# Where the weight pieces of a fused mLSTM and SwiGLU kernel land: other homes for pieces 2 to 6, and one half moved from ACT's queue to SP's

## The chip, the cores and the metric

The kernel runs on one core of a Trainium2 chip. Its engines are TensorE (PE in the profile; PEld is its weight load), VectorE (DVE), ScalarE (ACT), GpSimd (POOL) and SyncE (SP). Sixteen DMA engines move data; in this kernel the transfers are issued by SP (queue q1 of the profile) and by ACT (queue q10). The metric is the device time in microseconds (us), the median over runs.

## The reference

Two blocks follow each other. The first is an mLSTM cell over 4 batches, 8 heads, 768 positions and a head size of 40. The second is a SwiGLU block on 3072 tokens of 320 features, with 1536 hidden features.

```python
for t in range(S):
    m_new = np.maximum(f_gate[:, :, t] + m, i_gate[:, :, t])
    f_stab = np.exp(f_gate[:, :, t] + m - m_new)
    i_stab = np.exp(i_gate[:, :, t] - m_new)
    C = f_stab[..., None, None] * C + i_stab[..., None, None] * np.einsum('bhd,bhe->bhde', vt, kt)
    n = f_stab[..., None] * n + i_stab[..., None] * kt
    h_tilde = np.einsum('bhde,bhe->bhd', C, qt)
    denom = np.maximum(np.abs(np.einsum('bhd,bhd->bh', n, qt)[:, :, None]), 1.0)
    y[:, :, t] = h_tilde / denom / (1.0 + np.exp(-o_gate[:, :, t]))
x = y.transpose(0, 2, 1, 3).reshape(B * S, H * D)
g = x @ w_gate
out = (g / (1.0 + np.exp(-g)) * (x @ w_val)) @ w_out
```

The weights w_gate, w_val (320 x 1536) and w_out (1536 x 320) are numbers of 64 bits; the kernel computes with 32.

## The kernel before, in words

**Chunks.** The 768 positions are cut into six chunks of 128 (g = 0 to 5). For a chunk, the attention part yields x for 512 tokens (4 batches of 128 positions). The SwiGLU part then makes 12 *hidden steps* (m = 0 to 11, `hidden`, L648): 20 matmuls each, ten into a bank for the gate and ten into a bank for the value, with 64 features of the contraction on partitions 0 to 63 (gate weights) and 64 to 127 (value weights). ACT applies Silu to the gate bank (L653, into sg), VectorE multiplies with the value bank (L654) and writes slot m of h_sb, the memory of the gated products. That releases the two banks. There are four such banks, so hidden step m uses the banks of step m-2. After 12 steps, `project` or `project_all` (L664, L671) multiplies with w_out.

**Order.** The order of the work is written out by hand: each engine executes its instructions in the order of the program, and a semaphore holds an instruction until its inputs are there and its memory is free. While chunk 0's hidden steps run on TensorE, the attention of chunk 1 is worked in between them (`slots`, from L727). The steps that matter here: k and q of chunk 1 are loaded after step 0, turned on TensorE after steps 5 and 6 (`turn`, L296); w_sb is filled after step 2 from M_dram, a table of 80 KB that the kernel has written to HBM, with two broadcasting loads (L447); VectorE subtracts from w_sb after step 6 and after step 7 (`weights_sub`, L451), POOL masks it (L456), ACT takes the exponential after step 8 (L460).

**Chunk 0 ahead of that.** W0 (the decay weights of chunk 0) lies in slots 0 to 7 of h_sb, of 13. `first_own(u)` (L530) multiplies it with the values of batch u, reading slots 2u and 2u+1. M_of, a table for W0, lies in wo_sb, where the output weights come later. `burn` is a run of matmuls without use. `first_x`, `first_gate` and `first_seam` make x of chunk 0 and turn it into xT, with copies by ACT and VectorE (L121, L123).

**Weight pieces.** The 64-bit weights come in 10 *pieces*. Pieces 0 and 1 hold one hidden block of 128 features each (block 0, block 1). Pieces 2 to 6 hold two each (piece 2 blocks 2 and 3, up to piece 6 with blocks 10 and 11). Pieces 7 to 9 hold w_out, two blocks each (12 to 17), over all 128 partitions. A piece of w_gate and w_val consists of two transfers, a *half* each: the gate half to partitions 0 to 63, the value half to partitions 64 to 127. From piece 2 on, a half is 640 KB in runs of 2 KB. The halves are issued by two queues or by one (`queues` in `piece_load`, L165). A piece lands in raw, a ring of two buffers, or in memory handed in as `home`.

**Conversion.** A block is turned into 32-bit numbers by `scale` (ACT, L190 top and L192 low), `join` (VectorE, L199 and L200) and `rounded` (POOL or VectorE, L207). A `convert` does all three. Block m+2 is converted at the head of hidden step m for m up to 3, then blocks 6; 7 and 8; 9; 10; 11 at the heads of steps 4 to 8. ACT and VectorE thus do conversions, sg and products in one order.

**Queues.** Each transfer uses one of eight semaphores in turn, so that its issue also waits for the landing of the transfer eight before it. An issue that waits holds up all behind it on its engine. After piece 5, SP issues in this order: M_dram, k and q of chunk 1, piece 6, w_sb, v, piece 7, piece 8, o_sb, q of chunk 2 in 16 parts, piece 9.

Of the kernel before, what the change touches and what calls it, by code (L numbers as in the profile page):

```python
# [24 lines left out]
def kernel(  # L25
# [18 lines left out]
    nc = tc.nc  # L44
# [12 lines left out]
    NKC = DM // HP  # L57
    UH = BH // 2
    UA = UH // 2
    NH = NFC + 1  # L60
# [15 lines left out]
    def bank(name, tag="cell"):  # L76
        return psum.tile([128, 512], F32, name=name, tag=tag)
# [23 lines left out]
    wo_sb = const.tile([128, NFC, DM], F32)  # L101
    h_sb = const.tile([128, NH, TW], F32)
# [37 lines left out]
    def piece_load(p, home=None):  # L140
        kind, m, n = PIECES[p]
        if kind == "gv":
            a, d = NKC, n * 128
            src = [(slice(i * HP, (i + 1) * HP), w[:, m * 128:(m + n) * 128].rearrange("(c p) f -> p c f", p=HP))
                   for i, w in enumerate((moe_w_gate, moe_w_val))]
            queues = (nc.sync, nc.scalar if p < 5 else nc.sync)
        else:
            a, d = n, DM
            src = [(slice(0, 128), moe_w_out[m * 128:(m + n) * 128].rearrange("(a p) d -> p a d", p=128))]
            queues = (nc.sync,)  # L150
        if src[0][1].dtype == F32:
            for r, w in src:
                if kind == "o":
                    nc.sync.dma_start(out=wo_sb[r, m:m + n, :], in_=w)
                else:
                    for x in range(n):
                        nc.sync.dma_start(out=wgv_sb[r, m + x], in_=w[:, :, ts(x, 128)])
            return
        if home is None:
            raw = conv.tile([128, 4 * NKC * 128], U32, name="raw")  # L160
        else:
            raw = home.rearrange("p a t -> p (a t)").bitcast(U32)
        raw = raw[:, 0:2 * a * d]
        for (r, w), queue in zip(src, queues):
            queue.dma_start(out=raw[r].rearrange("p (a d) -> p a d", a=a), in_=w.bitcast(U32))  # L165
        words = raw.rearrange("p (a d two) -> p a d two", two=2, a=a)
        raws[p] = (words[:, :, :, 0], words[:, :, :, 1])
        split(p)
# [4 lines left out]
    def split(p):  # L173
        if p in raws:
            lo, hi = raws.pop(p)
            kind, m, n = PIECES[p]
            if kind == "gv":
                for c in range(n):
                    r = slice(c * 128, (c + 1) * 128)
                    blocks[m + c] = (lo[:, :, r], hi[:, :, r], wgv_sb[:, m + c])  # L180
            else:
                for c in range(0, n, 2):
                    blocks[NFC + (m + c) // 2] = (lo[:, c:c + 2], hi[:, c:c + 2], wo_sb[:, m + c:m + c + 2, :])
# [11 lines left out]
    def join(j):  # L195
        if j in blocks:
            lo, top, dst = blocks[j]
            both = dst.bitcast(U32)
            nc.vector.tensor_scalar(both, top, scalar1=3, scalar2=None, op0=ALU.logical_shift_left)  # L199
            nc.vector.scalar_tensor_tensor(both, in0=top, scalar=0x80000000, in1=both, op0=ALU.bitwise_and,  # L200
                                           op1=ALU.bitwise_or)
            blocks[j] = (lo, dst.bitcast(I32))
# [259 lines left out]
    def sig(P):  # L462
        nc.scalar.activation(o_sb[:, heads(P)], o_sb[:, heads(P)], AF.Sigmoid)


    def burn(n, tag="cell"):
        t = bank("burn", tag)
        for _ in range(n):
            nc.tensor.matmul(t, lhsT=junk[:, 0:128], rhs=junk, start=True, stop=True)
# [57 lines left out]
    def first_own(u):  # L527
        first_y[u] = bank("first_y", "gen")[:, 0:H * D1].rearrange("p (h d) -> p h d", d=D1)
        for h in range(H):
            nc.tensor.matmul(first_y[u][:, h, :], lhsT=W0[:, u * H + h, :], rhs=v_sb[:, u * H + h, :], start=True, stop=True)  # L530

    def first_x(u):
        y = first_y.pop(u)
        den = work.tile([128, UH, 1], F32, name="den")[:, 0:H]
        nc.vector.tensor_scalar(den, y[:, :, D:], scalar1=1.0, scalar2=None, op0=ALU.max)
        nc.vector.scalar_tensor_tensor(den, in0=y[:, :, D:], scalar=-1.0, in1=den, op0=ALU.mult, op1=ALU.max)
        nc.vector.reciprocal(den, den)
        nc.vector.tensor_tensor(x_sb[:, u, 0:DM].rearrange("p (h d) -> p h d", d=D), y[:, :, 0:D],
                                den.to_broadcast([128, H, D]), op=ALU.mult)

    def first_gate(P):
        for u in (2 * P, 2 * P + 1):
            x = x_sb[:, u, 0:DM].rearrange("p (h d) -> p h d", d=D)
            nc.vector.tensor_tensor(x, x, o_sb[:, u * H:(u + 1) * H], op=ALU.mult)
        nc.gpsimd.tensor_copy(x_sb[:, 2 * P:2 * P + 2, DM:], x_sb[:, 2 * P:2 * P + 2, 0:HP])
# [33 lines left out]
    first_turn(1, q_sb, qT, (A, V))  # L579
    load(o_sb, o_gate, 0, 1)  # L580
    piece_load(0)
    piece_load(1)
    late_maxima()
    first_own(1)
# [2 lines left out]
    first_x(1)  # L587
    sig(0)
    sig(1)
    piece_load(2, h_sb[:, NH - NKC:])  # L590
    piece_load(3, wo_sb)
    burn(3)
    first_own(2)
    first_own(3)
    first_gate(0)
    first_x(2)
    first_x(3)
# [1 line left out]
    scale(0)  # L599
    first_gate(1)  # L600
    burn(6, "gen")
    piece_load(4)
    join(0)
    first_seam(1, (A, A, V))
    rounded(0, V)
# [111 lines left out]
    def load_all(dst, a, n):  # L717
# [3 lines left out]
    run = lambda f, *a: (lambda: f(*a))  # L721
# [4 lines left out]
    ahead.update({4: [6], 5: [7, 8], 6: [9], 7: [10], 8: [11], 9: [], 10: [], 11: []})  # L726
    slots = {  # L727
        0: [run(first_state, 1, A), run(load_all, k_sb, k, 1), run(load_all, q_sb, q, 1)],
        1: [run(piece_load, 6, h_sb[:, NH - NKC:]), run(decay_rows)],
        2: [run(late_turns), run(weights_load, 1), run(load_all, v_sb, v, 1)],  # L730
        3: [run(decay)],
        5: [run(turn, 0, (A, A), (A, V))],
# [113 lines left out]
```

## Time and profile before

| what | us |
|---|---|
| median of 3 runs | 555.79 (554.63 to 557.81) |
| the profiled execution | 555.16 |
| its span, first to last instruction | 553.0 |
| TensorE busy in the span | 546.4 |
| hidden steps, L648 (1440 matmuls) | 317.3 |
| projection, L664 and L671 (576 matmuls) | 157.4 |
| first hidden step starts | 31.9 |

The span is what the profile's times count from; the time of an execution has 2.2 us around it. A line of a group or a timeline names the source line, engine, operation and what is written and read, then times. A wait is put down to what released it last. "Landing" of a transfer is the time at which its semaphore is complete; the DMA view gives the time from issue to landing. Landings of this stage, worked out from issue and duration:

| half | queue | issued | landed |
|---|---|---|---|
| piece 0 gate | SP | 19.23 | 28.4 |
| piece 2 gate, value | SP, ACT | 22.94, 25.43 | 33.4, 39.0 |
| piece 3 gate, value | SP, ACT | 23.69, 26.07 | 37.7, 42.7 |
| piece 4 gate, value | SP, ACT | 30.26, 30.04 | 41.4, 48.2 |
| piece 5 gate, value | SP, SP | 33.49, 37.72 | 46.0, 50.3 |
| piece 6 gate, value | SP, SP | 53.54, 55.89 | 63.0, 66.3 |

### The profile page before, as it was taken

The page shows a single profiled execution, that of the slowest core. Times are in us where ns is not written, and L with a number is a line of the kernel's source. Part 1 is how long each engine was busy: PE and PEld are TensorE (multiplying, and loading weights), DVE is VectorE, ACT ScalarE, POOL GpSimd, SP SyncE. Part 2 cuts the span into 40 slices and gives each one's busy share as a digit, 9 for nine tenths or more (in the row PEclk, how much of TensorE's full clock was granted, in tenths as well). Part 3 has the DMA queues.
Part 4 walks back from the last instruction along what each step waited for, and adds up shares of the span by engine and source line. Part 5 has one row for each costly group of instructions (what it writes and reads, how often), then busy time and mean ns, then how long its engine had stood idle before and what let it go on. Part 6 is the DMA issues. An engine that isn't in the chain of part 4 may idle for free.

```text
span 553.0 us, 11595 instructions
## 1 busy us (share of the span) xinstructions
PE 546.4 (99%) x4992; PEld 312.9 (57%) x4992; DVE 234.4 (42%) x394; ACT 134.7 (24%) x202; POOL 106.6 (19%) x97
## 2 busy tenths in 40 slices
PE   8999999999999999999999999999999999999997
PEld 4955546675545575544576455466455567444475
DVE  5956687962156332445521445531426621011100
ACT  4366564443101033110124101005110100111100
POOL 2314355574011151011133001114001200000000
PEclk9999999999999999999999999999999999999999
DMA  9999996798631763660464451395000131000000
GB/s 125 177 280 187 192 274 115 155 111 125 68 49 17 108 109 83 71 76 5 82 127 104 53 68 27 49 149 107 13 1 2 29 62 43 12 1 0 2 24 24
DMA packets 223994, 45.69 MB, mean 83 GB/s; under 512 B 214504, under 2 KB 219112, under 8 KB 223944
## 3 DMA queue, kind: packets, MB, share of 16 engines
q1 hardware_dynamic: 222036, 42.11, 46.7%
q10 hardware_dynamic: 1908, 2.85, 2.0%
q8 instruction: 39, 0.64, 0.5%
q14 instruction: 11, 0.09, 0.1%
HBM read 35.68 MB, written 4.01 MB: 72 GB/s over the span
## 4 chain that ended last, share of the span: by engine, by line
PE 92%; DMA 4%; SPq 3%; POOL 0%; DVE 0%; ACT 0%; issue 0%; ACTq 0%; POOLq 0%
PE gv_ps L648 55%; PE o_ps L664 24%; PE o_ps L671 5%; SPq L117 3%; DMA h_sb<-in_moe_w_val_dram 2%; PE inter L377 2%; PE sp L331 2%; PE intra L382 2%; DMA o_sb<-in_o_gate_dram 2%; PE add L353 1%; PE tp_kq L296 0%; POOL wgv_sb L207 0%; PE tp_x L439 0%; DVE wgv_sb L200 0%; ACT top L190 0%
## 5 line engine op out<-in xcount | busy, mean ns | idle before, releaser
L648 PE MATMUL gv_ps<-xT,wgv_sb 64*128 64x512 f32 x1440 | 317.3, 593 | 1.6 <-POOL wgv_sb L207 1.1
L648 PEld LDWEIGHTS gv_ps<-xT,wgv_sb 64*128 64x128 f32 x1440 | 139.1, 187 | 159.4 <-issue 154.6
L654 DVE TENSOR_TENSOR h_sb<-sg,gv_ps 128x512 f32<-128x512 f32 x72 | 49.5, 687 | 214.5 <-ACT sg L653 214.4
L664 PE MATMUL o_ps<-wo_sb,h_sb 128*128 128x320 f32 x480 | 130.5, 433 | 0.0
L664 PEld LDWEIGHTS o_ps<-wo_sb,h_sb 128*128 128x128 f32 x480 | 90.8, 190 | 41.0 <-issue 3.8
L653 ACT ACTIVATE sg<-gv_ps 128x512 f32<-128x512 f32 x72 | 43.0, 597 | 268.6 <-PE gv_ps L648 268.5
L362 POOL TENSOR_TENSOR C<-C,dec 128x328 f32<-128x328 f32 x20 | 14.5, 735 | 137.7 <-DVE C L369 137.6
L456 POOL TENSOR_SCALAR_AFFINE_SELECT w_sb<-w_sb 64x1024 f32<-64x1024 f32 x20 | 27.8, 1388 | 60.2 <-DVE w_sb L451 59.3
L658 ACT COPY z_sb<-o_ps 128x320 f32<-128x320 f32 x24 | 10.0, 422 | 94.7 <-PE o_ps L664 90.9
L403 POOL TENSOR_TENSOR o_sb<-o_sb,y_sb 128x640 f32<-128x640 f32 x10 | 14.3, 1428 | 79.2 <-DVE y_sb L394 79.1
L671 PE MATMUL o_ps<-wo_sb,h_sb 128*128 128x320 f32 x96 | 26.9, 437 | 0.0
L451 DVE TENSOR_TENSOR w_sb<-g_T,w_sb 128x1024 f32<-128x1024 f32 x10 | 13.2, 1355 | 27.6 <-DMA w_sb<-M_dram 27.6
L426 DVE STREAM_TRANSPOSE xT<-x_sq 128x640 f32<-128x640 f32 x16 | 12.5, 822 | 23.7 <-DMA x_sq<-x_sb 23.7
L671 PEld LDWEIGHTS o_ps<-wo_sb,h_sb 128*128 128x128 f32 x96 | 17.9, 190 | 7.2
L394 DVE TENSOR_TENSOR y_sb<-y_sb,intra 64x328 f32<-64x328 f32 x40 | 19.7, 493 | 0.8 <-PE intra L382 0.2
L369 DVE TENSOR_TENSOR C<-C,add 40x328 f32<-40x328 f32 (+1 forms) x36 | 17.7, 493 | 1.3 <-PE add L353 0.4
L207 POOL TENSOR_TENSOR wgv_sb<-wgv_sb,low 128x640 int32<-128x640 int32 x8 | 12.3, 1541 | 23.7 <-DVE wgv_sb L200 21.9
L377 PEld LDWEIGHTS inter<-C,qT 64*64 64x64 f32 x640 | 10.2, 134 | 7.3 <-issue 6.1
L341 POOL TENSOR_TENSOR vw_sb<-v_sb,w_sb 128x656 f32<-128x656 f32 x10 | 12.8, 1303 | 0.4
L338 DVE TENSOR_TENSOR w_sb<-sp,w_sb 128x512 f32<-128x512 f32 x20 | 12.7, 682 | 0.0
L460 ACT ACTIVATE w_sb<-w_sb 128x1024 f32<-128x1024 f32 x10 | 10.6, 1058 | 8.8 <-POOL w_sb L456 8.8
L397 DVE TENSOR_SCALAR den<-den 128x16 f32<-128x16 f32 x10 | 12.2, 1216 | 0.3
(129 smaller groups left out, 343.7 us busy)
## 6 DMA issues: line engine op xcount, KB each, us to landing
w_sb<-M_dram SPq DMA_DIRECT2D x10, 512.0 KB, 7.2
x_sq<-x_sb SPq DMA_DIRECT2D x128, 40.0 KB, 2.0
k_sb<-in_k_dram SPq DMA_DIRECT2D x12, 320.0 KB, 6.1
v_sb<-in_v_dram SPq DMA_DIRECT2D x12, 320.0 KB, 5.7
o_sb<-in_o_gate_dram SPq DMA_DIRECT2D x12, 320.0 KB, 5.4
raw<-in_moe_w_out_dram SPq DMA_DIRECT2D x3, 1280.0 KB, 7.8
out_dram<-z_sb SPq DMA_DIRECT2D x24, 160.0 KB, 1.8
q_sb<-in_q_dram SPq DMA_DIRECT2D x32, 64.0 KB, 2.4
```

Source lines behind the costliest of these rows:

```text
L117: nc.sync.dma_start(out=dst[:, heads(P), 0:D], in_=tokens(a, c, P))
L362: nc.gpsimd.tensor_tensor(state(s + 1)[:, a], state(s)[:, a], dec[:, s - 2, a].unsqueeze(2).to_broadcast([128, UA, D1]), op=ALU.mult)
L369: nc.vector.tensor_tensor(c, c, ps[r], op=ALU.add)
L377: nc.tensor.matmul(inter[two][half(i), a, :], lhsT=qT[half(two), P * UA + a, half(i)], rhs=state(2 * n + i)[half(two), P * UA + a, :], sta ...
L394: nc.vector.tensor_tensor(t, t, intra[i][half(c)], op=ALU.add)
L403: eng.tensor_tensor(o, o, y[:, :, 0:D], op=ALU.mult)
L456: nc.gpsimd.affine_select(w, w, compare_op=ALU.is_ge, fill=NEG, base=0, pattern=[[0, UH], [1, SUB]], channel_multiplier=-1)
L648: nc.tensor.matmul(ps[i], lhsT=wgv_sb[half(i), m, PAIRS[kc][i] if g < 2 else kc, :], rhs=x[half(i), kc, :], start=(kc == 0), stop=(kc == N ...
L653: nc.scalar.activation(sg, ps[0], AF.Silu)
L654: nc.vector.tensor_tensor(hid(g, m), sg, ps[1], op=ALU.mult)
L664: nc.tensor.matmul(p, lhsT=hid(g, m)[:, ts(u, L)], rhs=wo_sb[:, m, :], start=(m == 0), stop=(m == NFC - 1))
L671: nc.tensor.matmul(ps[u], lhsT=hid(g, m)[:, ts(u, L)], rhs=wo_sb[:, m, :], start=(m == 0), stop=(m == NFC - 1))
```

## The change

Piece 2 goes to slots 1 to 5 of h_sb instead of 8 to 12 and is issued behind first_own(2), piece 3 to slots 6 to 10 instead of wo_sb and behind first_own(3). Piece 4 goes to wo_sb instead of raw, and both of its halves are issued by SP, where ACT issued the value half. Pieces 5 and 6 take the two buffers of raw; before, pieces 4 and 5 had them, and piece 6 had slots 8 to 12 of h_sb. Pieces 7 to 9 follow in the ring: piece 7 now gets the buffer of piece 5 (before, of piece 4), piece 8 that of piece 6 (before, of piece 5). What TensorE, VectorE and POOL execute stays in the same order; ACT has one issue fewer and reads blocks from other places; SP has one issue more.

```diff
-            queues = (nc.sync, nc.scalar if p < 5 else nc.sync)
+            queues = (nc.sync, nc.scalar if p < 4 else nc.sync)
...
     sig(0)
     sig(1)
-    piece_load(2, h_sb[:, NH - NKC:])
-    piece_load(3, wo_sb)
     burn(3)
     first_own(2)
+    piece_load(2, h_sb[:, 1:1 + NKC])
     first_own(3)
+    piece_load(3, h_sb[:, 1 + NKC:1 + 2 * NKC])
+    piece_load(4, wo_sb)
     first_gate(0)
     first_x(2)
     first_x(3)
...
     first_gate(1)
     burn(6, "gen")
-    piece_load(4)
     join(0)
...
-        1: [run(piece_load, 6, h_sb[:, NH - NKC:]), run(decay_rows)],
+        1: [run(piece_load, 6), run(decay_rows)],
```

## The prediction

> **What bounds the kernel now.** I read the page's head first, then what TensorE waited for, the chain in order of time up to 130 us, the DMA view cut into short windows, and last the timeline of VectorE and TensorE around hidden steps 7 to 9. The head of the page (busy us, share of the span, instructions), and the three largest of TensorE's waits over the whole span (us in total, times, longest):
>
> ```profile
> span 553.0 us, 11595 instructions
> ...
> PE 546.4 (99%) x4992; PEld 312.9 (57%) x4992; DVE 234.4 (42%) x394; ACT 134.7 (24%) x202; POOL 106.6 (19%) x97
> ```
>
> ```profile
> PE burn L469 <- DVE warm L224: 1.2, 1, 1.2
> PE gv_ps L648 <- POOL wgv_sb L207: 1.1, 1, 1.1
> PE gv_ps L648 <- DVE m_in L285: 0.5, 1, 0.5
> ```
>
> TensorE is occupied throughout. An earlier weight load can remove at most the second line; everything else that the change can do to the time is a new wait. The chain around that line (start us, us, what):
>
> ```profile
> 25.43 13.59 DMA h_sb<-in_moe_w_val_dram
> ...
> 39.17 0.81 ACT top L190
> ...
> 41.51 1.54 POOL wgv_sb L207
> ...
> 43.10 4.80 PE gv_ps L648 x20
> ```
>
> Piece 2's value half is issued at 25.43, lands 13.6 us later, and is turned into block 2 by ACT, VectorE and POOL. Hidden step 2 starts at 43.10 where step 1 had ended at 42.0. Its 20 matmuls take 4.80 us instead of the usual 4.49, since its second bank comes free only at 43.29. The two losses make 1.4 us.
>
> The DMA view says why 640 KB took so long. Three windows: 28.5 to 32.5 (SP's queue q1 alone, gate half of piece 2), 34 to 44 (q1 with gate halves, ACT's queue q10 with value halves), 58.5 to 63 (q1 alone, gate half then value half of piece 6).
>
> ```profile
> DMA packets 409, 0.80 MB, mean 199 GB/s; under 512 B 17, under 2 KB 24, under 8 KB 409
> ```
>
> ```profile
> DMA packets 1734, 3.38 MB, mean 338 GB/s; under 512 B 84, under 2 KB 84, under 8 KB 1734
> ...
> q10 hardware_dynamic: 885, 1.73, 54.3%
> q1 hardware_dynamic: 849, 1.64, 51.2%
> ```
>
> ```profile
> DMA packets 465, 0.92 MB, mean 204 GB/s; under 512 B 16, under 2 KB 16, under 8 KB 465
> ```
>
> A half piece (64 partitions) alone moves at 199 GB/s, two opposite halves on two queues at 338 together, and two halves behind each other on one queue at 204. ACT's queue moved almost nothing between 26 and 32.8 us, although piece 2's value half had been issued.
>
> Later, VectorE waits for the broadcast of M_dram (start, us, engine and line, operation, [idle before]):
>
> ```profile
> 70.97 1.22 DVE L451 TENSOR_TENSOR w_sb<-g_T,w_sb 128x1024 f32<-128x1024 f32 x1 [1.31 <-DMA w_sb<-M_dram]
> ...
> 75.87 0.68 DVE L654 TENSOR_TENSOR h_sb<-sg,gv_ps 128x512 f32<-128x512 f32 x1
> ```
>
> ```profile
> 68.54 13.10 PE L648 MATMUL gv_ps<-xT,wgv_sb 64*128 64x512 f32 x60
> ```
>
> The 60 matmuls are steps 7, 8 and 9, so step 9 starts at 68.54 + 2/3 of 13.10 = 77.3. It writes the two banks of step 7, of which the second is released by the L654 at 75.87, done at 76.55. Its second matmul comes 0.2 us after its first, at 77.5: the slack is 0.9 us. That L654 stands behind L451 in VectorE's order. So w_sb has 0.9 us to spare before TensorE stops.
>
> [...] taking a half away from ACT's queue then has a price.
>
> **The change, part by part.**
>
> *Piece 2's home.* Its gate half now waits for the matmuls of first_own(2), which end at about 24.7 (32 matmuls of own(2) and own(3) in 22.88 to 26.54), so SP issues at 24.8 instead of 22.94. Piece 1's gate still moves until about 28.2, so q1 does not run dry. The value half stays at 25.43 on ACT. It is no longer issued behind both gate halves (22.94 and 23.69), only behind piece 2's. I take it that it starts about 1.2 us after piece 2's gate, as it now does after piece 3's (32.8 against 31.6): at 29.4, 3.7 us beside the other queue, 2 us to its semaphore, 35 us. Bounds: 33 (no delay at all) and 39.0 (as now). Block 2 is then ready by 39.3, before step 1 ends: TensorE gains 1.4 us there. With 39.0 it would gain nothing.
>
> *Piece 3's home.* It waits for first_own(3), 26.54. On SP only later pieces stand behind it. On ACT it goes at 26.6 instead of 26.07, and the two copies of xT behind it start at 27.3 instead of 27.04. Behind these stands the top of block 0, which waits for piece 0's landing (28.42) anyway: nothing. If that cover were gone, 0.25 us. Later hidden steps now write slots from which pieces 2 and 3 were read; ACT has read them before it makes the sg of those steps, so nothing.
>
> *Piece 4 on SP alone.* ACT loses a 0.6 us issue at 30.04, and its xT copies for the first hidden step come that much earlier. The step waits as well for block 0, which VectorE rounds until 31.76: gain 0.1 at most. SP gets one more half. After piece 1, q1 now carries five halves (2, 3, 4, 5 gate, 5 value), 3.28 MB: 11.4 us beside q10 (32.8 to 44.2) at 164 GB/s carry 1.87, the other 1.41 take 7.1 us at 199; 28.2 + 18.5 = 46.7, as seen (q1's 2 KB packets thin out at 47). Afterwards it carries six, 3.93 MB. q10 has two halves, 1.31 MB, 7.6 us at 173; beside them q1 moves 1.25 to 1.33 MB, and the remaining 2.60 to 2.69 take 12.8 to 13.4 us at 204 to 199: 20.4 to 21.0 us. The stream behind piece 5 is 1.9 to 2.5 us later; I take 2.2. Bounds: 1.3 if piece 4's and 5's halves overlap on the engines, 3.3 if the whole extra half (655 KB at 199) is paid.
>
> *What stands behind it on SP.* M_dram, k and q of chunk 1 (two each), piece 6, w_sb (two), v (two), pieces 7 and 8: the same order as now. The second k's issue lasts 10.5 us from 39.53, until just before piece 5's value half lands (50.26), and from 50.5 to 70 the queue is never empty. So 2.2 us are passed on whole. k and q: needed at 62.2 and 67.6 minus 1.4, landing at 56.5 (q, first half) and 60.3 (q, second) plus 2.2: covered by more than 2 us. Piece 6: lands 66.3 + 2.2 = 68.5, its block 10 starts on ACT at 69.67 - 1.4 = 68.3: 0.2 us of ACT, no TensorE. The second w_sb: VectorE's L451 goes from 70.97 to 73.2, and what follows it with it: L654 of step 7 ends at 76.55 + 2.2 = 78.75. Step 9, which would be ready at 77.5 - 1.4 = 76.1, gets its bank at 78.8: a new wait of 2.7 us, on L648 for VectorE's h_sb. Net: 78.8 - 77.5 = 1.3 us later than now; the early gain is swallowed, for step 9 starts by the load, not by TensorE.
>
> *Pieces 5 and 6 in the raw ring.* Piece 5 waits for block 0's scale (30.0, before piece 4 is through on SP), piece 6 for block 1's (33.5): nothing. Piece 8 needs piece 6's buffer, free only after block 11's low on ACT (75.87, 2.2 later by then) instead of block 9's: SP issues it at 78.1, not 72.25. Behind it o_sb and q's squares slip by some 3 us; o_sb is used at 97.99, landing 85.2 now; the squares are turned late in project_all. Hidden; if not, up to 3 us.
>
> *After step 9* everything on VectorE and POOL is 2.2 us later and TensorE 1.3. The tightest case is the add of chunk 1, whose banks the weighing frees at 86.9 for 88.1: 1.2 - 0.9 leaves 0.3 us. No further loss.
>
> Sum: -1.4 + 2.7 = +1.3 us. The profiled execution took 555.16 us (span 553.0 and 2.2 around), so 556.5; the median of the runs is 555.79, 0.6 above it, so 557.1 us.
>
> **Rivals.**
> 1. *The gain stays* (lateness of w_sb under 0.9 us): if the earlier start of q10 shortens q1 more than counted, or the idle gap at 49 to 50.5 swallows it. Against: the gap ends with piece 5's landing and moves with it. 554.4 to 555.7 us, the low end with all of the 1.4 gained.
> 2. *Slower beyond measure*: the pairing of halves breaks, [...] because piece 2 and 3 go out in another order. q10's 1.31 MB then take 6.6 us at 199 out of q1's own time: 28.2 + 19.7 + 6.6 = 54.5, lateness 7.4, net +6.5: 562. It decides from a lateness of 3.7 us on. For it: the DMA engines are 90% busy or more until 47 us. Against: 338 GB/s for 10 us in this very stage.
> 3. *Nothing changes*: piece 2's value half still starts at 32.8 and the queue ends as now: 555.8.
>
> **How the numbers follow.** Likeliest, 0.68: the wait moves from step 2 to step 9, with lateness 1.3 to 3.3, net +0.4 to +2.4, 556.2 to 558.2 us, point 557.1. Rival 1: 0.15. Rival 2, in degrees: 0.14. Rival 3: 0.03. A measurement of this kernel can tell about 0.5% (2.8 us) from no change. Faster beyond that needs more than the waits shown: 0.04. Slower: rival 2 and the upper edge of the first case, 0.19. Same: 0.77. The range 554.6 to 559.3 leaves out the lower tip of rival 1 and most of rival 2.
>
> **What would show it.** Right: TensorE's wait on L648 for POOL is gone and one for VectorE's h_sb of 2 to 3 us stands at 76; VectorE's L451 waits 3 us or more for w_sb; q10 carries 0.66 MB less, and starts its value halves before 31 us; q1 alone near 200 GB/s from 37 to 49. Wrong: no wait at step 9, or ACT still waiting for piece 2 until 39, or a wait at steps 3 to 8.

## The result, and the profile after

The changed kernel took 559.56 us (median of 17 runs, 557.48 to 561.89) against 555.48 us for the kernel before (17 runs of the same session): a ratio of 1.0077, 95% interval 1.0062 to 1.0092. That is 4.1 us slower. The prediction was 557.1 us with a range up to 559.3, and it gave most of the chance to a change within 0.5%: it was wrong in the size of the loss. The profiled execution took 559.34 us, with a span of 557.1.

The head of the changed kernel's page:

```profile
span 557.1 us, 11600 instructions
...
PE 550.1 (99%) x4991; PEld 313.4 (56%) x4992; DVE 233.5 (42%) x394; ACT 134.8 (24%) x202; POOL 106.8 (19%) x97
```

TensorE is busy for 3.7 us more (550.1 against 546.4) with the same work. Idle time alone can't be the answer, then: some matmuls took longer. Its three largest waits (us in total, times, longest):

```profile
PE gv_ps L648 <- DVE h_sb L654: 2.0, 1, 2.0
PE burn L469 <- DVE warm L224: 1.2, 1, 1.2
PE gv_ps L648 <- DVE m_in L285: 0.3, 1, 0.3
```

The wait for POOL at hidden step 2 (1.1 us) is gone, as predicted, though not by the change alone (see the point on step 2 near the end). A wait of 2.0 us for VectorE's product has come, also as predicted. Where it stands, in the chain around hidden step 9 (start us, us, what):

```profile
60.81 13.52 DMA w_sb<-M_dram
...
74.35 1.23 DVE w_sb L451
...
79.25 0.69 DVE h_sb L654
...
79.98 6.25 PE gv_ps L648 x18
86.23 2.02 PE sp L331 x128
```

The second transfer into w_sb lets L451 start at 74.35; step 7's product follows it on VectorE (L654) and frees the bank for the value, into which step 9's value matmuls go. Two things are to be seen in the last lines. L451 is 3.4 us later than before (70.97), where 2.2 were predicted. And the 18 matmuls take 6.25 us, though 20 of them normally take 4.49.

Why they take so long is seen when the span is cut into stretches of 3.41 us, the length of the half clock that this trace has from 80.78 to 84.19 (busy us and instructions of PE, PEld, DVE, ACT, POOL; then the granted clock, DMA share, GB/s):

```profile
77.36:80.78 3.42, 1.43 (x6) 0.49 (x6) 3.28 (x4) 3.02 (x4) 1.30 (x1) 1.00 0.97 343
80.78:84.19 3.41, 3.41 (x10) 1.39 (x8) 3.24 (x4) 1.28 (x3) 2.96 (x2) 0.50 0.93 342
```

In the first stretch TensorE worked for only 1.43 of 3.42 us, because of the wait. In the next one, all of it, TensorE was granted half its clock. This costs half of 3.41 us, 1.70 us. There is one more such stretch, at 26.16 to 29.58; its start lies 54.61 us before 80.78, which is 16 times 3.413. It costs nothing here: the hidden steps start 1.4 us later (33.29), but step 7 starts at 68.33 (before: 68.54), since the kernel before spent that time in its waits at step 2. Eight of the 13 profiles of this case have such an early stretch and five have none; it comes and goes with the same program. In the run called hold below, the kernel before has it too: start at 33.49, step 7 at 68.53. And of 72 runs of the kernel before, the 31 with a mean clock of 1.0 have a median of 555.1 us, the 27 with 0.997, 554.9 (one stretch at half clock, half of 3.41 us in 553, takes 0.003 off the mean).

The DMA view, three windows: 31 to 34, 34.5 to 38 and 38.5 to 50 us.

```profile
DMA packets 311, 0.63 MB, mean 210 GB/s; under 512 B 11, under 2 KB 11, under 8 KB 310
...
q10 hardware_dynamic: 276, 0.55, 92.1%
q1 hardware_dynamic: 34, 0.06, 10.1%
```

```profile
DMA packets 600, 1.19 MB, mean 341 GB/s; under 512 B 18, under 2 KB 18, under 8 KB 600
...
q10 hardware_dynamic: 298, 0.60, 52.3%
q1 hardware_dynamic: 302, 0.59, 51.9%
```

```profile
DMA packets 1227, 2.41 MB, mean 210 GB/s; under 512 B 57, under 2 KB 57, under 8 KB 1226
...
q1 hardware_dynamic: 1208, 2.37, 104.8%
```

From 31 to 34 us ACT's queue q10 brings piece 2's value half, and SP's q1 is nearly empty, although SP had issued piece 3's gate half at 27.10 and piece 4's at 27.74. Only piece 3's halves run beside each other (341 GB/s). The prediction had let both value halves on q10 run beside q1. By the bytes, that is enough for the lateness. In the kernel before, 3.38 MB went at 338 GB/s between 34 and 44 us; here 1.19 MB went at 341. An estimate: the 2.2 MB between them cost 4.5 us more at 200 GB/s than at 340; 3.3 us were seen (piece 5, below).

To see where each run gains and loses, I cut the span at points that are read from TensorE's timeline: the start of hidden step 7, the start of L331 after step 9 (chunk 1's scores), and the start of L331 of chunk 2. Differences to the kernel before, in us, each from one profile:

| run | until step 7 | steps 7 to 9 | to chunk 2 | rest | span |
|---|---|---|---|---|---|
| before (the times themselves) | 68.54 | 13.03 | 63.20 | 408.27 | 553.0 |
| after | -0.2 | +4.8 | -0.6 | +0.1 | +4.1 |
| p4_both | +1.1 | +0.2 | +0.9 | +0.1 | +2.3 |
| only_sp | -0.7 | +2.6 | +0.7 | -0.1 | +2.5 |
| burn_step9 | -0.2 | +2.7 | +3.1 | 0.0 | +5.6 |
| sub_later | +0.2 | 0.0 | +0.8 | 0.0 | +1.0 |
| gates_first | +0.6 | +3.4 | +1.1 | 0.0 | +5.1 |
| hold | 0.0 | +1.0 | +0.6 | 0.0 | +1.6 |
| hold5 | -0.7 | +5.3 | -0.3 | 0.0 | +4.3 |
| value_early | 0.0 | 0.0 | -0.5 | 0.0 | -0.5 |

The rest, three quarters of the span, is the same in all to 0.25 us. The changed kernel's loss lies in steps 7 to 9. Its 4.8 us are 1.70 for the half clock and 3.1 for the wait. The wait is listed with 1.99, but costs 1.1 more: in the kernel before a gate and a value matmul, on opposite halves of the partitions, start as a pair every 0.43 us (in step 9 at 77.18 and 77.61); at 76.97 and 77.40 two gate matmuls went alone, while the value bank was still held.

This splits the loss of the profiled execution, not of the median. Of the 17 runs, six had a mean clock of 0.994 or less (0.994 in the profiled one, which has two stretches at half clock) and a median of 560.2 us; ten had 0.997, by the same measure one stretch, and 559.2. The mean does not tell where in the span a stretch lay.

### The profile page after: what moved, and what is told of

It reads as the page before. It is cut to its first block, busy times and chain, and to the rows that moved or that the text cites. A ratio compares the mean times of both kernels' runs of the same rounds, so it can differ in the third digit from the quotient of the medians.

```text
span 557.1 us, 11600 instructions
## 1 busy us (share of the span) xinstructions
PE 550.1 (99%) x4991; PEld 313.4 (56%) x4992; DVE 233.5 (42%) x394; ACT 134.8 (24%) x202; POOL 106.8 (19%) x97
## 4 chain that ended last, share of the span: by engine, by line
PE 95%; DMA 2%; DVE 1%; ACT 0%; issue 0%; SPq 0%; ACTq 0%; DVEq 0%
PE gv_ps L648 54%; PE o_ps L664 23%; PE o_ps L671 5%; DMA w_sb<-M_dram 2%; PE inter L377 2%; PE sp L331 2%; PE intra L382 2%; PE add L353 1%; PE first_y L530 1%; PE burn L469 1%; PE tp_x L561 1%; PE tp_kq L509 1%; PE sp L519 1%; PE wps L480 0%; PE wps L484 0%; PE wps L489 0%
## 5 line engine op out<-in xcount | busy, mean ns | idle before, releaser
L654 DVE TENSOR_TENSOR h_sb<-sg,gv_ps 128x512 f32<-128x512 f32 x72 | 49.4, 687 | 219.6 <-ACT sg L653 217.6
L658 ACT COPY z_sb<-o_ps 128x320 f32<-128x320 f32 x24 | 10.0, 422 | 95.6 <-PE o_ps L664 91.8
L451 DVE TENSOR_TENSOR w_sb<-g_T,w_sb 128x1024 f32<-128x1024 f32 x10 | 13.2, 1355 | 31.0 <-DMA w_sb<-M_dram 31.0
L207 POOL TENSOR_TENSOR wgv_sb<-wgv_sb,low 128x640 int32<-128x640 int32 x8 | 12.3, 1537 | 21.9 <-DVE wgv_sb L200 21.9
L190 ACT ACTIVATE top<-raw 128x640 f32<-128x640 f32 x12 | 9.6, 798 | 11.9 <-issue 5.3
```

Source lines behind the costliest of these rows:

```text
L451: nc.vector.tensor_tensor(w_sb[:, heads(P)], gb, w_sb[:, heads(P)], op=ALU.subtract)
L654: nc.vector.tensor_tensor(hid(g, m), sg, ps[1], op=ALU.mult)
```

## The experiments

In the diffs, lines are cut to what was changed. The ratios are to the kernel before on the same chip.

**Each part alone.** p4_both is the changed kernel with piece 4 again behind the second burn and on both queues; only_sp is the kernel before with nothing but piece 4's value half moved to SP.

```diff
 # p4_both, against the changed kernel
-queues = (nc.sync, nc.scalar if p < 4 else nc.sync)
+queues = (nc.sync, nc.scalar if p < 5 else nc.sync)
-piece_load(4, wo_sb)          # behind piece_load(3, ...)
+piece_load(4, wo_sb)          # behind burn(6, "gen")
 # only_sp, against the kernel before
-queues = (nc.sync, nc.scalar if p < 5 else nc.sync)
+queues = (nc.sync, nc.scalar if p < 4 else nc.sync)
```

> The changed kernel, but piece 4's value half goes back to ACT's queue, at the place in the order where it was before (behind the scale of block 0); the new homes of all pieces stay. Theory (the extra half on SP's queue makes w_sb late, and TensorE waits at hidden step 9): SP carries five halves again, VectorE's wait before L451 falls from 4.9 us to under 2.5, TensorE's wait before step 9 falls from 2.0 us to under 0.5, the half-clock stretch at 81 us goes; 554.0 to 556.0 us, ratio to before 0.996 to 1.001. Rival (the later issue of pieces 2 and 3, behind first_own, is to blame, since SP's queue ran dry from 31 to 34 us): the dry stretch stays, so most of the lateness stays: wait at step 9 of 1 us or more, 557 us or more.

> The kernel before, and only this of the change: piece 4's value half is issued by SP, right behind its gate half; homes and places in the order as before. Theory (the extra half on SP): w_sb 2 to 3.3 us later than before, a wait before step 9 of 1.1 to 2.4 us, with or without half clock after it; step 2 keeps its 1.1 us wait for POOL; 557 to 559.5 us, ratio 1.002 to 1.007. Rival (homes and later issue are to blame): no wait at step 9, ratio 0.998 to 1.001.

p4_both took 556.77 us, ratio 1.0026 (1.0011 to 1.0041); only_sp 557.17 us, 1.0041 (1.0024 to 1.0058). L451 came at 72.69 and 73.44, so 1.7 and 2.5 us late; the change as a whole, 3.4 us late, does worse than either. only_sp came out as its theory had it: the moved half alone makes w_sb late and TensorE wait.

p4_both is mixed. The wait and the half clock at step 9 are gone, as the theory said (+0.2 in the table), yet the time is above 556.0: its profile loses ahead of step 7 (+1.1) and in the lead-in to chunk 2 (+0.9, a gap at L382, see below). And it is late from the start. ACT waited for o_sb's load until 27.70 us (25.42 before, 24.62 after), and issued the value halves of pieces 2 and 3 only behind that. So how much of its 1.7 us comes from the new homes is not shown.

In only_sp step 9 waits, and still the clock stays up:

```profile
PE gv_ps L648 <- DVE h_sb L654: 1.5, 1, 1.5
```

Its steps 7 to 9 lose 2.6 us: 1.5 listed and again 1.1 for matmuls that went alone. The stretch with the wait, its borders reckoned back in steps of 3.413 us from a half clock at the end of the trace (an estimate; in the changed kernel's trace the half clock at the end, 558.65, begins 140 such steps behind 80.78):

```profile
75.67:79.08 3.41, 1.89 (x10) 0.58 (x6) 3.27 (x4) 2.23 (x4) 2.01 (x2) 1.00 0.92 320
```

TensorE was busy for 1.89 us of it, and full clock followed.

**The wait without any transfer changed.** hold and hold5 are the kernel before with extra passes of VectorE behind the first L451. They multiply half of w_sb by one, so the results stay.

```diff
+def hold():
+    for _ in range(3):        # hold5: 5
+        nc.vector.tensor_scalar(w_sb[:, heads(1)], w_sb[:, heads(1)], scalar1=1.0, scalar2=None, op0=ALU.mult)
-6: [..., run(weights_sub, 1, 0), run(weights_mask, 0), run(piece_load, 7)],
+6: [..., run(weights_sub, 1, 0), run(weights_mask, 0), run(piece_load, 7), run(hold)],
```

> The kernel before with no transfer changed: three extra passes of VectorE over the second half of w_sb (multiplied by one, about 1.0 us each) are put behind the first L451, so that step 7's product in L654 comes about 3 us later, as in the changed kernel, by VectorE alone. By the trace of the kernel before the product would end at 76.55 + 3 = 79.6, and step 9's second matmul, which started at 77.5, would wait about 2.1 us. Theory A (a wait of 2 us alone is what drops TensorE's clock, and a stretch of 3.41 us at half clock follows): a wait of 2 us and then 2 us lost at half clock, 559 us. Theory B (the wait costs itself; the half clock of the changed kernel came from elsewhere): 557.2 us and no stretch at half clock behind the wait. Theory C (the step has slack elsewhere): 555 us.

hold missed its aim: 557.17 us, 1.0039 (1.0025 to 1.0054), with no listed wait and no half clock behind step 9. The product ended at 78.04, only 1.5 us later than before, because L200 and L207, which followed, took 0.83 us each (from 75.66) instead of 1.64 and 1.54 (from 72.64 in the kernel before). There POOL's mask ran from 72.27 to 75.28; in hold it was done at 74.67. Steps 7 to 9 lost 1.0 us: matmuls went alone at 77.17 and 77.60. So the cost begins before the list shows a wait. The median is the number of theory B, but by luck: the wait that the three theories are about did not arise.

> The kernel before, no transfer changed, with five instead of three extra passes of VectorE over the second half of w_sb behind the first L451. With three, step 7's product ended at 78.04 and steps 7 to 9 took 14.05 us instead of 13.03, without a listed wait. Two more passes of 0.7 to 1.5 us each put the product's end at 79.5 to 81, so that step 9's second matmul waits 2 to 3.5 us and steps 7 to 9 take 15.5 to 17 us at full clock, 557.5 to 559 us. Theory A [...]: the times fall into two bunches 1.5 to 2 us apart, with the mean clock lower by 0.003 in the upper one, and a profile with a half clock after the wait has its start a whole number of 3.41 us from the one near 26 us. Theory B [...]: one bunch, no half clock behind the wait.

hold5 took 559.39 us, ratio 1.0066 (1.0048 to 1.0084), within 0.2 us of the changed kernel, with every transfer issued as before. TensorE's wait, and the stretches around it (columns as above):

```profile
PE gv_ps L652 <- DVE h_sb L658: 2.5, 1, 2.5
```

```profile
77.36:80.77 3.41, 0.88 (x5) 0.49 (x6) 3.24 (x5) 2.25 (x4) 0.00 (x0) 1.00 1.07 372
80.77:84.18 3.41, 3.41 (x10) 1.39 (x8) 3.24 (x4) 2.03 (x2) 2.96 (x2) 0.50 0.93 157
```

(L658 is the product, four lines further down in this kernel.) 2.5 + 1.1 + 1.7 make the 5.3 us of the table. The product ended at 79.97, in the changed kernel at 79.92. Of its six runs, four had a mean clock of 0.997 and took 559.25 to 559.48 (the profiled one is among them, with the stretch above); one with 0.999 took 557.3; one with 0.994 took 560.19. So a late product of step 7, by VectorE alone, is enough for the whole loss. That the clock makes the 2 us between 557.3 and the four others fits theory A, but rests on one run, of which there is no trace.

**What makes the product late.** sub_later is the changed kernel with the first weights_sub and its mask moved from step 6 to step 7, behind that step's product. All transfers stay.

```diff
-6: [run(turn, 1, (A, A), (A, V)), run(weights_sub, 1, 0), run(weights_mask, 0), run(piece_load, 7)],
-7: [run(weights_sub, 1, 1), run(weights_mask, 1), run(nc.gpsimd.memset, q_sb, 0.0)],
+6: [run(turn, 1, (A, A), (A, V)), run(piece_load, 7)],
+7: [run(weights_sub, 1, 0), run(weights_mask, 0), run(weights_sub, 1, 1), run(weights_mask, 1), run(nc.gpsimd.memset, q_sb, 0.0)],
```

> The changed kernel with one move in VectorE's and POOL's order: the first subtraction from w_sb and its mask (L451, L456) come after hidden step 7's product (L654) instead of before it, next to the second ones. The loads are untouched. Theory (w_sb's late landing reaches TensorE only because that product stands behind the subtraction): w_sb is as late as in the changed kernel, but there is no wait before step 9 and no half clock at 81 us; the early gain at step 2 remains: 553.5 to 555.0 us, ratio to before 0.996 to 0.999. Rival (the lateness holds TensorE by another way as well, through the exponential, the scores or the adds): a wait of 1 us or more at a later step, 557 us or more.

It took 555.01 us, ratio 1.000 (0.9988 to 1.0012): the wait and the half clock at step 9 are gone, as the theory said. The early gain at step 2 that it counted on does not show (step 7 starts at +0.2 in the table). VectorE's timeline:

```profile
73.92 0.69 DVE L654 TENSOR_TENSOR h_sb<-sg,gv_ps 128x512 f32<-128x512 f32 x1 [0.89 <-ACT sg L653]
74.52 2.35 DVE L451 TENSOR_TENSOR w_sb<-g_T,w_sb 128x1024 f32<-128x1024 f32 x2
```

w_sb is as late as in the changed kernel, and it costs nothing, since the product no longer stands behind it. The control before_sub_later makes the same move in the kernel before:

> The kernel before with only the first weights_sub and its mask moved from step 6 to step 7, behind that step's product. Theory A (in the kernel before this wait sets nothing, since step 9's second matmul follows its predecessor at once): 555.1 us, and the move is worth its full 4.5 us only in the changed kernel. Theory B (the move helps whatever the stream of weights does): 553.5 us or less.

556.33 us, ratio 1.0016 (1.0004 to 1.0028): there the move gains nothing, and is even a little slower (its profile has a TensorE gap of 1.17 us at L382, below). So the changed kernel's loss goes through L451's place in VectorE's order. No version that I ran beats the kernel before; sub_later equals it.

**The half clock by itself.** burn_step9 is the changed kernel with eleven useless matmuls put ahead of step 9, into the wait.

```diff
-            run(piece_load, 8)],
+            run(piece_load, 8), run(burn, 11)],      # end of slots[8]
```

> The changed kernel, and 11 matmuls without use (2.4 us) on TensorE ahead of hidden step 9, where it waits 2.0 us for VectorE. They take no time from the path while the wait is there. Theory (the wait lets the clock fall to half for one stretch of 3.4 us, which costs step 9 another 2.1 us): the clock stays at 1.0 from 60 us on, step 9's matmuls take 4.5 us instead of 6.3, and the time is 1.5 to 2.3 us less than the changed kernel's, 557.0 to 558.0 us, ratio to before 1.003 to 1.005. Rival (the half clock is a matter of load or chance and not of the wait): no gain, 559.5 us or a little more, ratio 1.007 to 1.009.

559.14 us, ratio 1.0072 (1.0055 to 1.009): no gain in sum. Steps 7 to 9 did gain 2.1 us and had the full clock, but the lead-in to chunk 2 lost 3.8 against the changed kernel. Even the seven of its 19 runs with a mean clock of 0.999 or more have a median of 558.5 us. In the profile TensorE stood still once more, in the second attend, and a stretch at half clock followed (104.98 to 108.4). Its timeline:

```profile
102.43 0.54 PE L382 MATMUL intra<-v_sb,w_sb 64*64 64x41 f32 x23
104.90 1.35 PE L382 MATMUL intra<-v_sb,w_sb 64*64 64x41 f32 x41 [1.94 <-issue]
```

"issue" means that the profile knows no wait for it. The gap stands after the 23rd of 64 matmuls; in the other runs that have it, after the 34th. With 11 matmuls more ahead of it, that is the same number of instructions, about 2212 from TensorE's start. So the gap stands at one place in the stream of instructions. The page lists a queue q8 of the kind "instruction", with 39 transfers in a run and 0.64 MB, so 16 KB in each. That they bring TensorE's instructions is my inference. Where the fetch on q8 before the gap began, against piece 9's data (1.3 MB of output weights on all partitions), in us:

| run | piece 9's data | fetch begins | gap at L382 |
|---|---|---|---|
| value_early | 93.9 to 98.1 | 97.9 | none |
| sub_later | 98.2 to 105.6 | 97.9 | none |
| before | 94.2 to 98.5 | 98.3 | 0.33 |
| hold | 95.2 to 99.7 | 99.6 | 0.45 |
| value_sub | 97.5 to 102.9 | 100.2 | 0.84 |
| only_sp | 97.0 to 101.3 | 101.1 | 0.90 |
| before_sub_later | 95.1 to 99.4 | 99.1 | 1.17 |
| p4_both | 96.8 to 101.0 | 100.7 | 1.25 |
| gates_first | 99.7 to 104.9 | 103.7 | 1.45 |
| burn_step9 | 98.4 to 103.8 | 102.6 | 1.94 |
| after | 98.5 to 102.9 | 102.4 | none |
| hold5 | 96.2 to 100.5 | 101.4 | none |

The matmuls behind the gap start 2.3 to 2.6 us after the fetch begins. In the changed kernel itself (and in hold5) TensorE reaches this place 4.6 us later than before, and the fetch is in time. In all but sub_later and hold5 the fetch begins in the last 1.2 us of piece 9's data, or in value_sub amid them, as if it had waited for them.

burn_fetch tests this: burn_step9 with piece 9 issued behind the load of w_sb for chunk 2.

```diff
-11: [run(do_attend, 1, 0), run(do_gather, 1, 0, False), run(piece_load, 9)],
+11: [run(do_attend, 1, 0), run(do_gather, 1, 0, False)],
-1: [run(do_gather, 1, 1), run(weights_load, 2), run(load_all, v_sb, v, 2)],
+1: [run(do_gather, 1, 1), run(weights_load, 2), run(piece_load, 9), run(load_all, v_sb, v, 2)],
```

> The kernel with eleven useless matmuls ahead of step 9, and besides it piece 9 (1.3 MB of output weights) issued behind the load of w_sb for chunk 2 instead of ahead of it, some 10 us later. Without this second edit TensorE stood still for 1.9 us at the second attend's L382 for nothing that the trace names, and then had 3.4 us at half clock; the fetch [...] had been under way among piece 9's packets. Theory A (the fetch waits behind piece 9's data): the gap at L382 falls to under 0.3 us, no half clock follows, 555.6 us. Theory B (the gap has another cause): gap and half clock stay, 559 us or more.

The gap is gone:

```profile
103.34 1.13 PE L382 MATMUL intra<-v_sb,w_sb 64*64 64x41 f32 x64
```

The fetch began at 100.1, with no data of piece 9 about (110.5 to 114.8). The time was not better: 561.65 us, ratio 1.0098 (1.007 to 1.0126, four runs). Piece 9 now comes too late for its conversion on ACT, whose copies of xT TensorE then waits for:

```profile
117.62 1.37 PE L439 MATMUL tp_x<-ident,x_sb 64*128 64x64 f32 x20 [1.23 <-ACT xT L121]
```

A stretch at half clock follows this wait too (119.35 to 122.76; 27 times 3.413 us after the one at 27.19). So the fetch theory held in this pair of profiles, and the expected time did not.

**Why the stream is 3.4 us late.** gates_first is the changed kernel, with the value halves of pieces 2 and 3 issued by ACT only behind its copies of the first seam.

```diff
-    piece_load(2, h_sb[:, 1:1 + NKC])
+    piece_load(2, h_sb[:, 1:1 + NKC], held)                 # ACT's issue goes into the list held
-    piece_load(3, h_sb[:, 1 + NKC:1 + 2 * NKC])
+    piece_load(3, h_sb[:, 1 + NKC:1 + 2 * NKC], held)
     first_seam(0, (A, A, V))
+    for go in held:
+        go()
```

> The changed kernel, but ACT issues the value halves of pieces 2 and 3 only behind its copies of the first seam, at about 29 us instead of 24.97 and 27.11, so that on the chip the gate halves of pieces 2, 3 and 4 are issued first, as the kernel before issues those of 2 and 3 first. Theory A (a half begins when what was issued before it, on either queue, has nearly gone out; the changed order gate 2, value 2, gate 3 left SP's queue empty from 31.2 to 33.9): SP's queue has data without a gap from 27.7 on, the first L451 comes at about 72 us instead of 74.4, the wait before step 9 is under 0.5 us, but block 2 is late again, with a wait on GpSimd of 1 to 2 us at step 2; 555.5 to 557 us. Theory B (SP's queue runs dry whatever the order on ACT): the gap stays, L451 at 74 us or later, 559 us.

Neither theory held: 560.7 us, ratio 1.0092 (1.0067 to 1.0117). SP's queue did have data without a gap, as A said, but L451 came at 75.40, not at 72. (The profiles of after, burn_step9 and burn_fetch, with one order of transfers until then, have it at 74.35, 73.65 and 74.89; so that it is later than in the changed kernel says little.) What kept it late shows in the window from 40.2 to 43.4:

```profile
DMA packets 321, 0.65 MB, mean 202 GB/s; under 512 B 5, under 2 KB 5, under 8 KB 321
...
q1 hardware_dynamic: 162, 0.33, 54.1%
q10 hardware_dynamic: 159, 0.32, 53.2%
```

Both queues move, and yet it is only 202 GB/s: here, by their landings, q1 brings piece 4's value half and q10 piece 3's, both to partitions 64 to 127 (piece 3's two halves, to opposite partitions, ran at 341 in the changed kernel). p4_both has the same between 45.4 and 47.4, with the value halves of pieces 5 and 4:

```profile
DMA packets 201, 0.40 MB, mean 201 GB/s; under 512 B 5, under 2 KB 5, under 8 KB 201
```

Two such halves also come from one tensor, w_val. That one tensor as a source is not the limit is suggested by piece 9, which is one tensor on one queue, but goes to all 128 partitions (the kernel before, 94.5 to 98):

```profile
DMA packets 453, 1.16 MB, mean 331 GB/s; under 512 B 0, under 2 KB 0, under 8 KB 453
```

So in these windows two queues did not pay where both wrote to the same 64 partitions. The empty queue was not what cost most, but any half that had no opposite half at hand: in the changed kernel piece 2's value half (210 GB/s from 31 to 34 us) and, from 38.5 on, four halves in a row (210 again).

gates_first also tells something on the clock. Its step 9 waits longer than the changed kernel's, and the clock stays at 1.00:

(The lines of this kernel are seven further down.)

```profile
PE gv_ps L655 <- DVE h_sb L661: 2.2, 1, 2.2
```

```profile
76.30:79.71 3.41, 2.48 (x10) 0.76 (x6) 3.24 (x4) 0.92 (x2) 2.94 (x2) 1.00 0.98 227
79.71:83.13 3.42, 2.10 (x10) 1.07 (x12) 3.38 (x5) 3.37 (x4) 0.95 (x1) 1.00 0.90 314
```

The borders of these two stretches are reckoned back in the same way from the half clock at the end of that trace. The wait lies across both, so that TensorE is busy for 2.48 and 2.10 us of each.

value_early is the kernel before with pieces 2 and 3 issued between the two sigmoids, so that ACT issues their value halves early.

```diff
     sig(0)
-    sig(1)
     piece_load(2, h_sb[:, NH - NKC:])
     piece_load(3, wo_sb)
+    sig(1)
```

> The kernel before, but pieces 2 and 3 are issued between the two sigmoids, so that their value halves go to ACT's queue at about 22 us instead of 25.4, ahead of the gate halves of pieces 1 to 3 on SP's queue. Theory A (the order of issue over both queues decides when a half begins): the value half of piece 2 runs beside gate halves from about 26 us instead of 32.8, the stretch from 26 to 32.8 runs at over 300 GB/s instead of 196, the 1.1 us wait on GpSimd at step 2 goes, the first L451 is not late; 554.0 us. Theory B (the value half begins at 32.8 whenever it is issued): nothing moves, 555.0 us.

The mechanism is as in theory A: the window from 28 to 33 us, in which q10 had stood still,

```profile
DMA packets 858, 1.68 MB, mean 337 GB/s; under 512 B 34, under 2 KB 58, under 8 KB 856
...
q10 hardware_dynamic: 431, 0.85, 53.0%
q1 hardware_dynamic: 425, 0.81, 49.7%
```

and block 2 is ready at 40.88 instead of 43.04, so the wait at step 2 is gone. So in this run an earlier issue among those of both queues made the half move earlier (block 2 by 2.2 us); why the queues take turns in this way is not shown. The time is inconclusive: 556.5 us, ratio 1.0014 (0.999 to 1.0038), in two bunches around 554.8 and 558.3. value_sub, which adds sub_later's move to it, was to clear that up:

> The kernel before with two edits: pieces 2 and 3 issued between the two sigmoids, as in the run that did this alone, and the first weights_sub with its mask moved from step 6 to step 7, behind that step's product. The first edit alone gave times in two bunches, around 554.8 and around 558.3 us. Theory A (in the 558 bunch w_sb is late and step 7's product waits for L451): the upper bunch goes, 554.5 us. Theory B (the upper bunch has another cause, a late start of the hidden steps or a gap in the fetch of instructions): both bunches stay, 556 us.

557.66 us, ratio 1.0049 (1.0031 to 1.0066). It is slower, with times from 555.0 to 559.8, so a late w_sb is not what makes the upper bunch. What does stays open; no trace fell into it. The kept trace of value_sub (556.72 us, between the bunches) starts its hidden steps at 34.57 (value_early: 33.52) and has a gap of 0.84 us at L382, the two causes that theory B names.

The landing of piece 5's value half, the last of the stream, against L451, in us:

| run | piece 5 lands | L451 |
|---|---|---|
| value_early | 49.43 | 70.28 |
| before | 50.26 | 70.97 |
| p4_both | 51.60 | 72.69 |
| only_sp | 52.36 | 73.44 |
| after | 53.57 | 74.35 |
| gates_first | 53.84 | 75.40 |

L451 follows it by 20.7 to 21.6 us in all six: SP's order hands the lateness on whole, to within 0.9 us, as the prediction said.

## Why the prediction was wrong, point by point

- *The wait at step 2 goes*: right on the load. Piece 2's value half landed at 37 instead of 39 (35 was predicted; it started at 30.8, not 29.4), and block 2 was ready at 40.98, ahead of the 42.0 at which step 1 had ended before. But the 1.4 us of gain were read from one execution. hold, hold5 and before_sub_later have the transfers of the kernel before, and in them this half landed at 37.4 to 38.3; hold5 lists a wait of 0.3 us for POOL, the other two, whose hidden steps start 1.4 to 1.6 us later, none. So that no wait is listed in the changed kernel is in part chance, and the gain was smaller than the sum had it. As the sum said, it does not reach the end: step 9 starts by the load.
- *Piece 3's home, piece 5's and 6's ring, piece 8's later issue, k and q*: right; no wait of TensorE stands at steps 3 to 8 or in chunk 1's load. Piece 8 was issued at 79.23 (78.1 predicted), hidden.
- *"The stream behind piece 5 is 1.9 to 2.5 us later; I take 2.2"*: the first step that failed. It came 3.3 us later, and L451 3.4, the upper bound that I had given and not taken. (Three profiles with the changed kernel's transfers and three with those of the kernel before put L451 at 73.65 to 74.89 and 70.29 to 70.97: 2.7 to 4.6 us apart, in any case more than 2.2.) The sum let both of q10's value halves run beside q1 ("beside them q1 moves 1.25 to 1.33 MB"). Only piece 3's did. In place of "piece 2's value half starts about 1.2 us after piece 2's gate", the runs show that it moved when that gate had almost gone out, and that piece 3's gate waited for it in turn. The second rival, that the pairing breaks because the pieces go out in another order, had the right mechanism; its price (lateness 7.4; its own numbers, 54.5 less 46.7, give 7.8) assumed that both value halves on q10 lose their partner, and one did.
- *Passed on whole, net wait at step 9*: the mechanism was right, to the instruction. Its size follows from the lateness: the first value matmul came at 79.98, 2.8 us after 77.18 in the kernel before, where the prediction had 78.8 against 77.5. The slack was 0.6 us (76.55 to 77.18), not 0.9: in the kernel before the first gate and the first value matmul of step 9 start together, at 77.18, and not 0.2 us apart from 77.3.
- *"No further loss"*: the second step that failed. Half clock after the wait cost 1.70 us, which the sum did not have at all. A listed wait of 1.99 us, in a stretch in which TensorE was busy for 1.43 of 3.42 us, went ahead of it; the predicted wait was longer, 2.7 us.

From the predicted +1.3 to about the profile's +4.1: 1.2 more lateness, 0.3 less slack, 1.7 half clock, and 0.5 regained further on, of which 0.3 is the gap at L382. hold5 and sub_later show the first three together from both sides: the late product alone makes such a loss, and without it the late stream costs nothing. That one stretch of half clock is worth 1.7 fits two profiles, after and gates_first: their steps 7 to 9 differ by 1.4 us in favour of the run whose wait is 0.25 longer.

## What to carry to other kernels

A wait moved to another place must be priced with what TensorE's clock does behind it: here, in the profiled execution, a stop of 2 us cost 4.8, of which the list of waits shows 2.0. Before moving a transfer between queues, write down which transfers then run side by side and onto which partitions, in the order of issue over all queues; in these runs two halves gained only where they were opposite and at hand together (337 to 341 GB/s, against 199 to 210 otherwise). And look at what stands behind the instruction that will be late: moving one subtraction behind the product that TensorE waits for took the ratio from 1.0077 to 1.000. And read a wait of 1 us from more than one execution before counting it as a gain.

## What the runs showed of the hardware that I had not expected

- **Half clock came in stretches of 3.413 us.** In the changed kernel's trace two whole ones are 3.413 us long each and begin 54.61 us apart, 16 times that; in burn_step9 and burn_fetch two begin 23 and 27 times that apart. At step 9, and at L382 in burn_step9, a stretch with TensorE busy for 0.88, 1.43 or 1.47 us was followed by half clock; one with 1.89 (only_sp), 2.10 or 2.48 us (gates_first) was not. So a wait's length alone did not decide whether it cost 1.7 us more: that of 1.99 us did, that of 2.2 us in gates_first, which by the reckoned borders lies across two stretches, did not. Busy time as listed isn't all: the transposes' stretch in burn_fetch had 2.18 us and was followed by half clock, and so was a stretch ahead of 26.16 with 3.36 of 3.42 us, most of it matmuls of 41 columns (L530). What sets the clock was not shown.
- **A gap of TensorE beside a fetch of instructions.** TensorE stood still for 1.94 us in burn_step9, where a fetch of 16 KB began at 102.6 us amid a 1.3 MB load; the gap went when the load was moved (burn_fetch). This is one pair of profiles.
- **Halves to opposite partitions, and to the same.** 337 to 341 GB/s for a gate half beside a value half on two queues, 201 and 202 for two value halves on the same two queues.
- **VectorE beside GpSimd.** L200 took 1.64 us while POOL's mask ran (the kernel before: L200 at 72.64, mask from 72.27 to 75.28), 0.83 after it (hold: mask until 74.67, L200 at 75.66). In sub_later it took 0.83 us at 71.24, ahead of the mask, and 1.63 at 78.26, during it (75.81 to 80.89). This is read from traces; no run was made for it.
